# Loading the second sketch matrix through another engine's queue, and moving one group of products within the prologue

## Chip, cores and metric

One core of one Trainium2 chip. The metric is device time in microseconds (us) of one execution, the median of several. Most executions of one kernel agree within 0.3%; now and then one takes 193 to 196 us. These are called slow here and are left out of the comparisons.

## The reference, cut to what matters

```python
def phi(x):                                  # 64 features from two sketches of 8
    a = np.einsum('rd,bhsd->bhsr', S1, x)    # S1, S2: (8, 32)
    b = np.einsum('rd,bhsd->bhsr', S2, x)
    return np.einsum('bhsi,bhsj->bhsij', a, b).reshape(*x.shape[:-1], 64)
q_p, k_p = phi(q), phi(k)                    # q, k, v: (4, 4, 1088, 32)
kv, z = k_p^T v, sum(k_p)
attn = (q_p kv) / (q_p z + 1e-6)
x = attn.transpose(0, 2, 1, 3).reshape(4352, 128)
out = relu(x @ w_in)**2 @ w_out              # w_in (128, 2048), w_out (2048, 128)
```

Nothing can be computed before S1 and S2 are in SBUF: k and q both pass through them.

## The kernel before

Nearly all of the time is the feed-forward part, which TensorE does for chunk after chunk of tokens. Ahead of it stands a prologue for batch 0: load S1, S2 and the first pieces of k, q and v; turn the sketch matrices (`s_T`); compute k features (`kf`, two or three tiles of 128 tokens at a time); sketch 256 tokens of q in two steps (`q0(0)`, `q0(1)`); sum k features against v (`kvp`); divide; and feed the first tokens to the feed-forward part (`pg`, line L615). While the loads are under way, TensorE runs ten products on constants (`warm`), so that its clock is up when real work comes.

```python
    nc.vector.memset(s_nat[:], 0.0)
    nc.scalar.dma_start(s_nat[0:8, :], S1[:, :])        # L214
    nc.scalar.dma_start(s_nat[8:16, :], S2[:, :])       # L215
    load_k(nc.sync, 0, 0, 512)
    load_k(nc.sync, 0, 512, S)
    load_q(nc.sync, 0, 0, 256)
    ...
    load_v(nc.sync, 0, 0, 0, 4)
    load_v(nc.scalar, 0, 2, 0, 4)
    load_v(nc.sync, 0, 1, 0, 4)
    load_v(nc.scalar, 0, 3, 0, 4)
    ...
    keep_warm(W0)                                       # W0 = 10
    a_kT0(0, 4)                                         # VectorE transposes k, first chunk
    nc.vector.transpose(s_T[:, :], s_nat[:, :])         # L706, needs S1 and S2
    ...                                                 # copies of s_T into sf and sq
    a_kf(0, 2, psf, "po")
    a_kf(2, 2, psf, "pg")
    a_kf(4, 3, psf, "po")
    q0(0)
    q0(1)
    nc.scalar.copy(_ap(qb0, ...), banks(x0, 0, 0, 256))
    st[0, "kvp"] = psf.tile([128, 512], F32, tag="pg", name="kvp")
    for t0, n in ((0, 2), (2, 2), (4, 3), (7, 2)):
        a_kp0(t0, n)                                    # VectorE: kp = outer product of kf
        for t in range(t0, t0 + n):
            a_kv0(t)                                    # TensorE: kvp
        if t0 == 0:
            a_kf(7, 2, psf, "po")
```

## Time and profile before

| | before |
|---|---|
| first three runs | 189.06, 189.63, 195.55 us |
| profiled run | 189.23 us, span 187.4 us |
| TensorE busy | 182.0 us, 97% |
| prologue, to the first L615 product | 14.17 us |
| after it | TensorE never idle to speak of |

A line of the chain of waits gives start, duration and what ran; the chain is the work that ended last, followed back. A line of the timeline gives start, duration, engine, line, operation, and in square brackets how long the engine had been idle and what ended that. VectorE's timeline at the end of the k features:

```profile
9.62 0.69 DVE L322 TENSOR_TENSOR kp<-kf,kb 128x512 f32<-128x512 f32 x1 [1.21 <-ACT kb L312]
10.23 0.68 DVE L767 TENSOR_TENSOR qp<-x,qb 128x512 f32<-128x512 f32 x1
11.17 0.49 DVE L780 TENSOR_TENSOR bd<-kvp,own_p 128x128 f32<-128x128 f32 x2 [0.26 <-PE kvp L376]
```

VectorE waits 1.21 us for the last k features, which the change addresses.

### The profile page before, as it was taken

The numbers are of one execution on the slowest core, as the hardware profiler recorded it, in microseconds if no ns is written. First come the engines' busy times: TensorE is split into PE (matmuls) and PEld (weight loads), VectorE is DVE, ScalarE is ACT, GpSimd is POOL, SyncE is SP. The second block draws the span as 40 slices with busy tenths as digits, with TensorE's granted clock in tenths as the row PEclk, the third lists the DMA queues.
The fourth block names the chain that finished last, engine by engine and source line by source line (L and its number), as shares of the span: only waits on it lengthen the run. The fifth ranks groups of instructions, "written<-read, shape, count | busy, mean of one in ns | idle before, by whom it ended". The sixth has DMA issues, their size and how long they took to land.

```text
span 187.4 us, 4142 instructions
## 1 busy us (share of the span) xinstructions
PE 182.0 (97%) x1586; PEld 121.8 (65%) x1587; DVE 115.0 (61%) x261; ACT 149.4 (80%) x329; POOL 28.0 (15%) x125
## 2 busy tenths in 40 slices
PE   8999999999999999999999999999999999999991
PEld 2757866666656666656577666656577655666890
DVE  4779879958992589469944589469943412222400
ACT  3418778778978989789698989789698998999960
POOL 2832000028400000085000000085000000000000
PEclk9999999999999999999999999999999999999998
DMA  6799400100039600200069200200020200020101
GB/s 189 189 344 325 125 3 2 28 3 5 0 50 251 143 6 0 44 1 2 7 146 251 35 3 0 42 3 0 7 41 0 35 0 2 9 43 0 31 11 28
DMA packets 24411, 11.27 MB, mean 60 GB/s; under 512 B 17864, under 2 KB 22728, under 8 KB 24392
## 3 DMA queue, kind: packets, MB, share of 16 engines
q1 hardware_dynamic: 23940, 10.82, 23.7%
q8 instruction: 12, 0.20, 0.4%
q10 hardware_dynamic: 452, 0.20, 0.4%
q14 instruction: 7, 0.06, 0.1%
HBM read 8.78 MB, written 2.23 MB: 59 GB/s over the span
## 4 chain that ended last, share of the span: by engine, by line
PE 94%; DMA 2%; DVE 1%; issue 0%; ACT 0%; POOL 0%; ACTq 0%; DVEq 0%
PE po L653 60%; PE pg L615 18%; PE nd L538 3%; PE kvp L394 2%; PE pol L648 2%; PE po L648 2%; PE qc L296 2%; DMA s_nat<-in_S_dram 2%; PE kvp L376 1%; PE kf L306 1%; PE kc L296 1%; PE x L749 1%; PE nd L547 1%; PE den L795 0%; PE den L773 0%
## 5 line engine op out<-in xcount | busy, mean ns | idle before, releaser
L653 PE MATMUL po<-g,w_o 128*128 128x384 f32 (+3 forms) x352 | 138.4, 478 | 0.0
L615 PE MATMUL pg<-xT,w_in 128*128 128x384 f32 (+3 forms) x192 | 110.1, 582 | 0.3 <-DVE xT L810 0.3
L624 ACT ACTIVATE gt<-pg 128x384 f32<-128x384 f32 (+4 forms) x177 | 85.2, 489 | 20.0 <-PE pg L615 16.9
L653 PEld LDWEIGHTS po<-g,w_o 128*128 128x128 f32 x352 | 62.6, 189 | 22.3 <-issue 7.3
L632 ACT ACTIVATE g<-gt 128x384 f32<-128x384 f32 (+3 forms) x138 | 71.0, 532 | 2.9
L615 PEld LDWEIGHTS pg<-xT,w_in 128*128 128x128 f32 x192 | 36.0, 190 | 25.1 <-issue 7.2
L634 DVE TENSOR_TENSOR g<-gt 128x384 f32<-128x384 f32 (+4 forms) x39 | 21.4, 550 | 39.5 <-ACT gt L624 39.4
L443 POOL COPY kv<-kvt 32x64 f32<-32x64 f32 x48 | 11.8, 246 | 89.7 <-PE po L653 63.9
L506 DVE STREAM_SHUFFLE qa<-qc 128x576 f32<-128x576 f32 (+2 forms) x20 | 11.6, 650 | 0.0
L521 DVE TENSOR_TENSOR qp<-qa,qb 128x576 f32<-128x576 f32 (+2 forms) x20 | 10.8, 601 | 0.0
L497 POOL COPY rd<-rc 32x9 f32<-32x9 f32 x48 | 8.9, 185 | 2.2
L347 DVE TENSOR_TENSOR kp<-fs 128x576 f32<-128x576 f32 x12 | 8.2, 741 | 0.0
L469 DVE STREAM_TRANSPOSE qt<-qc 128x576 f32<-128x576 f32 x6 | 4.3, 762 | 5.5 <-PE qc L296 5.5
L657 DVE STREAM_TRANSPOSE oT<-po 128x384 f32<-128x384 f32 (+3 forms) x11 | 6.2, 560 | 1.2 <-PE po L653 1.2
L538 PE MATMUL nd<-qp,kv 32*32 32x288 f32 (+2 forms) x320 | 6.8, 353 | 0.0
L338 DVE STREAM_TRANSPOSE fs<-kc 128x576 f32<-128x576 f32 x6 | 4.3, 762 | 3.9 <-PE kc L296 3.9
L538 PEld LDWEIGHTS nd<-qp,kv 32*32 32x32 f32 x320 | 3.8, 103 | 3.5 <-issue 2.1
L584 DVE TENSOR_TENSOR xT<-nd,bc 128x576 fp32r<-128x576 f32 (+2 forms) x10 | 5.6, 596 | 0.8 <-PE nd L538 0.7
L506 DVE STREAM_SHUFFLE qb<-qc 128x576 f32<-128x576 f32 (+2 forms) x10 | 6.0, 648 | 0.0
L696 PE MATMUL warm<-const-bfloat16-1.0 128*128 128x512 bf16 x12 | 5.2, 585 | 0.8 <-PEq L1072 0.8
L289 DVE STREAM_TRANSPOSE qT<-qn 128x192 f32<-128x192 f32 (+3 forms) x11 | 5.8, 562 | 0.0
L575 DVE STREAM_TRANSPOSE bc<-rd 128x576 f32<-128x576 f32 (+2 forms) x10 | 5.7, 603 | 0.1
(98 smaller groups left out, 97.6 us busy)
## 6 DMA issues: line engine op xcount, KB each, us to landing
kn<-in_k_dram SPq DMA_DIRECT2D x3, 544.0 KB, 6.8
qn<-in_q_dram SPq DMA_DIRECT2D x3, 544.0 KB, 6.7
vn<-in_v_dram SPq DMA_DIRECT2D x9, 144.0 KB, 5.3
out_dram<-oT SPq DMA_DIRECT2D x24, 48.0 KB, 1.8
w_in<-in_moe_w_in_dram SPq DMA_DIRECT2D x4, 256.0 KB, 6.5
w_o<-in_moe_w_out_dram SPq DMA_DIRECT2D x4, 256.0 KB, 5.9
out_dram<-oT SPq DMA_DIRECT2D x8, 56.0 KB, 1.9
qn<-in_q_dram SPq DMA_DIRECT2D x1, 416.0 KB, 5.6
```

What stands on the lines that cost most here:

```text
L347: nc.vector.tensor_tensor(out=_ap(st[b, "kp"], 0, 128, 2 * o, [[64, NT], [8, 8], [1, 8]]), in0=_ap(fs, 0, 128, o, [[32, NT], [1, 8], [0, 8]]),
L443: nc.gpsimd.tensor_copy(_ap(st[b, "kv"], 32 * c, 32, 64 * h, [[32, E], [1, 32]]), _ap(st["kvt"], 32 * h, 32, 0, [[64, E], [1, 32]]),)
L497: nc.gpsimd.tensor_copy(st[b, "rd", 0][32 * h : 32 * h + 32, NT * c : NT * c + NT], st[b, "rc"][32 * c : 32 * c + 32, NT * h : NT * h + NT],)
L506: nc.vector.stream_shuffle(in_=banks(st[b, "qc", i0], 2 * x, 0, m), out=_ap(st[b, which, i0], 0, 128, 2 * m * x, [[m, 2], [1, m]]), mask=m ...
L521: nc.vector.tensor_tensor(out=st[b, "qp", i0, e][:, r], in0=st[b, f"qa{e}", i0][:, r], in1=st[b, "qb", i0][:, r], op=mult,)
L538: nc.tensor.matmul(nd[32 * h : 32 * h + 32, 512 * c + col : 512 * c + col + m], kv[r, o : o + 32], qp[r, m * h : m * h + m], start=(e == 0 ...
L615: nc.tensor.matmul(st["pg", u][:, n * i : n * i + n], w_in[:, 128 * (d0 + i) : 128 * (d0 + i) + 128], st[b, "xT"][:, c0 : c0 + n],)
L624: nc.scalar.activation(gt[:, 0:w], st["pg", u][:, 0:w], Relu)
L632: nc.scalar.activation(g2[:, 0:w], gt[:, 0:w], Square)
L634: nc.vector.tensor_tensor(out=g2[:, 0:w], in0=gt[:, 0:w], in1=gt[:, 0:w], op=mult)
L648: nc.tensor.matmul(po[x // 128][:, 0:128], g[:, x : x + 128], w, start=(d == 0), stop=(d == NB - 1),)
L653: nc.tensor.matmul(po[0][:, 0:n], w, g, start=(d == 0), stop=(d == NB - 1))
```

## The change

The intent has two parts. Part 1: S1 and S2 no longer share ScalarE's queue; S2 goes through GpSimd's, so both can start at once. Part 2: the last k features (`a_kf(7, 2)`) are computed between the two q sketches and not after the first `kvp` products, so VectorE gets them sooner.

```diff
-    nc.scalar.dma_start(s_nat[8:16, :], S2[:, :])
+    nc.gpsimd.dma_start(s_nat[8:16, :], S2[:, :])
@@
     q0(0)
+    a_kf(7, 2, psf, "po")
     q0(1)
@@
         for t in range(t0, t0 + n):
             a_kv0(t)
-        if t0 == 0:
-            a_kf(7, 2, psf, "po")
```

## The prediction

> **What bounds the kernel now.** I read the page first. Its busy line and its chain say the same thing.
>
> ```profile
> span 187.4 us, 4142 instructions
> ...
> PE 182.0 (97%) x1586; PEld 121.8 (65%) x1587; DVE 115.0 (61%) x261; ACT 149.4 (80%) x329; POOL 28.0 (15%) x125
> ...
> PE 94%; DMA 2%; DVE 1%; issue 0%; ACT 0%; POOL 0%; ACTq 0%; DVEq 0%
> ```
>
> TensorE carries 94% of the chain that ended last, and nearly all of it is the two feed-forward products (L653 and L615). The change touches none of those: comparing the instruction order of the two kernels, the only differences are in the first 14 us, plus a renumbering of the DMA semaphores. So the second view is busy time by stage, with a cut at 14.17 us, where the first L615 product starts.
>
> ```profile
> 0.00:14.17 14.17, 12.93 (x131) 7.66 (x132) 9.16 (x34) 4.62 (x13) 6.53 (x28) 1.00 0.81 241
> 14.17:24.00 9.83, 9.76 (x153) 7.87 (x154) 8.52 (x33) 8.06 (x16) 0.85 (x2) 1.00 0.74 210
> 24.00:60.00 36.00, 36.00 (x422) 22.02 (x421) 28.60 (x67) 29.25 (x63) 6.76 (x32) 1.00 0.17 38
> ```
>
> (Columns: stretch, length, busy TensorE, weight loads, VectorE, ScalarE, GpSimd.) After 14.17 TensorE is full (9.76 of 9.83, then 36.00 of 36.00). So what the prologue saves shifts everything after it by the same amount; nothing later is waiting to swallow it, and nothing later can be gained.
>
> Third, the chain inside the prologue, in order of time (start, duration):
>
> ```profile
> 1.53 2.89 DMA s_nat<-in_S_dram
> ...
> 4.52 0.21 DVE s_T L706
> ...
> 4.78 0.20 POOL sf L711
> 4.98 0.25 ACT sq L717
> ...
> 5.32 1.75 PE kf L306 x14
> 7.07 1.06 PE x L749 x8
> 8.13 0.61 PE kvp L376 x16
> 8.75 0.59 PE kf L306 x4
> 9.34 1.78 PE kvp L376 x56
> 11.12 0.58 PE den L773 x4
> ```
>
> Two things are to be seen. The sketch matrices decide when real work starts: their load lands at 4.42. Then TensorE goes from 5.32 to 11.12 with nothing but its own work on the chain. Fourth, the timeline shows what stands beside this load.
>
> ```profile
> 0.91 0.59 ACTq L214 DMA_DIRECT2D s_nat<-in_S_dram  x1
> ...
> 1.53 0.30 ACTq L215 DMA_DIRECT2D s_nat<-in_S_dram  x1
> ...
> 3.42 0.71 DVE L283 STREAM_TRANSPOSE kt<-kn 128x512 f32<-128x512 f32 x1 [1.13 <-DMA kn<-in_k_dram]
> ...
> 4.52 0.20 DVE L706 STREAM_TRANSPOSE s_T<-s_nat 32x32 f32<-32x32 f32 x1 [0.38 <-DMA s_nat<-in_S_dram]
> ```
>
> S1 is issued at 0.91, S2 behind it at 1.53. The trace's landing records separate them: S1's last landing is at 3.57, S2's at 4.42. S2, second on the same queue, is the late one. VectorE is idle for only 0.38 us because of it, since it transposes the first k chunk until 4.13.
>
> **What the Trainium skill says.** "DMA: Bandwidth & Descriptors", section "Issuing engines are not separate DMA queues": every queue ends on the same 16 engines, so issuing from another engine saves only sequencer time. Here that is S1's 0.59 us in front of S2, and S2 lands 0.85 us after S1, so the trace agrees that the order of issue costs something, and shows more than the issue time. The same page, section "SWDGE vs HWDGE vs iDMA" with the table "Specifications": the GpSimd queue builds its descriptors in software, with about 1 us to the first byte against about 0.6 us for ScalarE's. The trace of before has no kernel load from GpSimd, so this is untested; for ScalarE's queue it shows 1.71 us from S1's issue to its first packet (0.91 to 2.62), far over 0.6, with the k load moving beside it. "SBUF — State Buffer", section "Who interferes with whom": VectorE in a two-port mode locks GpSimd out of the ports it writes descriptors with. Before 3.42 VectorE runs only memsets here (none after 2.3), so I expect no block. "TensorE: Matmul & The Clock Gate", Part 1: the array runs at half clock until a free-running window of about 3.4 us has been busy. The trace agrees: the ten warm-up products start 0.43 us apart up to 4.57, and two later ones (13.08 and on) load 0.22 us apart; the recorded full clock begins at 5.03.
>
> **Part 1, S2 through GpSimd.** Removed: S2 from behind S1. Added: one load at the head of GpSimd's program, waiting for the 32x32 memset of VectorE that ends at 0.89, so issued near 0.92. How long it takes is the uncertain number. Estimate A: S1's issue-to-landing of 2.66 us (3.57-0.91) plus the page's 0.4 us difference in first byte: 0.92+3.06 = 3.98. Estimate B: the page's fixed 2.0 us for a small GpSimd load ("Anatomy of one DMA"): 2.9. I take 3.8, with 4.4 possible. S1 itself stays at about 3.57.
>
> What it buys is capped by VectorE: the k transpose ends at 4.13, so the transpose of the sketches can start at 4.15 to 4.17 rather than 4.52: 0.36 us. From there to the first kf product was 0.80 us (4.52 to 5.32): a 0.20 us transpose, two copies of 0.17 and 0.24 us on VectorE, and hops. That gives 4.96. The second cap is the warm-up: the tenth warm product starts at 4.57 and takes 0.43 us of the array, to 5.00. So kf starts at 5.00 instead of 5.32: **0.32 us saved**. The other inputs follow: the second k chunk landed at 4.25 and q at 5.06, before the shifted 4.85 and 5.61 at which VectorE wants them; v landed by 5.94 against a need near 8.
>
> GpSimd's memsets (0.31, 0.31, 0.12 us) move behind the load. If the load holds GpSimd 1 to 1.5 us, they end near 3.2, still before its first copy at 4.4. SP's loads were paced by waits on semaphores that S1 and S2 share with later v loads: one v load was issued at 4.44, right after S2 landed. Without S2 on these semaphores it goes near 3.9, and the loads behind it some 0.2 us sooner; all of them land ahead of their use already, so this is worth nothing.
>
> **Part 2, last k features between the two q sketches.** TensorE gets the same instructions in another order: kf 14 passes, sketch one, kf 4, sketch two, kvp 72, rather than kf 14, both sketches, kvp 16, kf 4, kvp 56. I price it from single starts in the trace. Before, the first kf to the first den product is 11.05-5.32 = 5.73 us. For the new order: kf to sketch 1.68 (5.32 to 7.00); sketch one, two pairs 0.32 apart, then 0.31 to the next kind (as 7.76 to 8.06): 0.63; four kf passes 0.16+0.11+0.11, then 0.20 to the next kind: 0.58; sketch two and change-over again 0.63; 72 kvp passes at 0.0292 us, from 1.63/56: 2.10; then 0.15 to den. Sum 5.77, **0.05 us more**: the sketch is split and its slower first pass is paid twice.
>
> What it gives is off the path. VectorE waited for the last k features:
>
> ```profile
> DVE kp L322 <- ACT kb L312: 1.2, 1, 1.2
> ```
>
> That product ran 9.62 to 10.31. In the new order kf ends near 8.3, its copy near 8.5, and the product near 9.2 (all before Part 1's shift). But its consumers, the last 16 kvp passes, began only at about 10.43 anyway; the 56 passes run at 29 ns with no gap, like the first 16. The qp product moves from 10.23 to about 9.3, and its consumer waits for the kvp sum (11.05 and the two bd products) regardless. The new kf needs a PSUM buffer freed by the first kp product at 6.95, and TensorE reaches it at about 7.6, so it does not stall. Part 2 alone: 0 to 0.05 us worse.
>
> **Sum.** -0.32 + 0.05 = -0.27 us, about 0.14%. Undisturbed runs of before gave 189.06, 189.63 and, profiled, 189.23: mean 189.3. Less 0.27 is 189.0; the median quoted for before (189.63) sits higher, so I say 189.1.
>
> **Rivals.** (1) *The GpSimd load lands later than 4.42.* For: software descriptors, the k load on all engines, GpSimd's slower start. Against: 3.5 us between issue and 4.42. At a landing of 4.9 the kernel becomes 0.5 us slower, 189.8. I give it 20%. (2) *Part 2 was the real aim and removes a TensorE stall.* For: VectorE's idle 1.2 us. Against: the gapless kvp passes. If right, with the 0.15 us or so of changing between kinds also saved, 188.8. 10%. (3) *The clock decides.* If the window falls so that the array warms later, the kf passes run at half speed, and part of the early start is lost: gain 0.15 instead of 0.32. It varies by run and not by kernel, so it is noise on both, perhaps 0.5 us. (4) *Earlier loads collide* and delay the w_in chunks: chunk three landed at 13.61 and is wanted after 16, so over 2 us of slack. Under 5%.
>
> **Range and chances.** Spread of before's good runs 0.6 us, the mechanism between -0.6 and +0.5: 188.4 to 189.9 holds 8 in 10. Two per cent is 3.8 us, which is fourteen times the effect; only a median that falls in the slow state (195.55 was seen) gets there, and verdicts leave that out.
>
> **What would show it.** Right: the sketch transpose starts at 4.1 to 4.2 with VectorE idle before it under 0.1 us or waiting for nothing; first kf near 5.0; kf to den 5.75 to 5.8; the last kp product with no idle before it; first L615 product near 13.9. Wrong: that transpose waits for the S2 load past 4.4; or kf to den shrinks below 5.6; or TensorE idles before the four kf passes; or the stretch from the first L615 product to the end changes by more than 0.3 us.

## The result, and the profile after

| | before | after |
|---|---|---|
| median | 189.32 us (6 runs) | 189.75 us (6 runs) |
| fast runs | 189.06 to 189.63 | 189.52 to 189.89 |
| ratio of fast runs | | 1.0024, interval 1.0010 to 1.0038 |
| span of the profiled run | 187.40 | 187.73 |
| last landing of S2 | 4.42 | 4.50 |
| sketch transpose starts | 4.52 | 4.52 |
| first `kf` product | 5.32 | 5.32 |
| first `kf` to first `den` | 5.73 | 5.90 |
| first `den` to first L615 | 3.12 | 3.12 |
| first L615 to last product | 168.89 | 168.91 |
| last landing of output to end of span | 0.96 | 1.10 |

Ratios are the mean time of one kernel's fast runs over that of the other's of the same rounds, so not quite the ratio of the medians. The change is within 2% and inside the predicted range, but its sign is the other way: 0.24% slower, where 0.14% faster was forecast.

The chain of waits of the changed kernel:

```profile
0.90 0.35 issue
1.25 3.25 DMA s_nat<-in_S_dram
4.50 0.02 issue
4.52 0.21 DVE s_T L706
...
5.32 1.87 PE kf L306 x14
7.19 0.63 PE x L749 x4
7.83 0.59 PE kf L306 x4
8.41 0.63 PE x L749 x4
9.05 2.25 PE kvp L376 x72
11.29 0.58 PE den L772 x4
```

The first line is new: between the end of VectorE's memset and the start of GpSimd's load lie 0.35 us in which nothing that the profile shows is waited for. The load then takes 3.25 us where S2 on ScalarE's queue took 2.89, so the 0.28 us of earlier issue (1.25 against 1.53) are gone, and the transpose starts at 4.52 as before. The rest runs as in the prediction's list of the new order: 0.63, 0.59, 0.63, 2.25. Only the first entry differs, 1.87 for 1.75.

VectorE's timeline of the changed kernel:

```profile
4.52 0.20 DVE L706 STREAM_TRANSPOSE s_T<-s_nat 32x32 f32<-32x32 f32 x1 [0.34 <-DMA s_nat<-in_S_dram]
...
8.70 0.69 DVE L322 TENSOR_TENSOR kp<-kf,kb 128x512 f32<-128x512 f32 x1 [0.18 <-ACT kb L312]
9.71 0.69 DVE L766 TENSOR_TENSOR qp<-x,qb 128x512 f32<-128x512 f32 x1 [0.32 <-ACT qb L760]
11.34 0.49 DVE L779 TENSOR_TENSOR bd<-kvp,own_p 128x128 f32<-128x128 f32 x2 [0.94 <-PE kvp L376]
```

The sketch transpose still waits for the load of S2. Part 2 does what it was meant to: the wait of 1.21 us is 0.18. It comes back two lines on, as a wait of 0.94 us for `kvp`; `bd` starts 0.17 us later than before.

Busy time by stage of the changed kernel, with the cut at its first L615 product (length, TensorE, weight loads, VectorE, ScalarE, GpSimd):

```profile
0.00:14.34 14.34, 13.13 (x130) 7.65 (x132) 9.35 (x34) 4.62 (x13) 7.40 (x29) 1.00 0.84 241
14.34:24.17 9.83, 9.77 (x153) 7.87 (x154) 8.52 (x33) 8.05 (x16) 0.62 (x1) 1.00 0.82 207
24.17:60.17 36.00, 36.00 (x422) 22.02 (x421) 28.63 (x67) 29.26 (x63) 6.81 (x32) 1.00 0.17 38
```

TensorE is as full as before. Matched product by product, the two kernels stand 0.18 us apart from the middle of `kvp` to the last product. So the 0.33 us of this pair of profiles are 0.18 in the prologue and 0.14 after the last product.

Three causes were in question. A: the route through GpSimd (a later S2, and something at the program's end). B: the new order on TensorE. C: chance, because the array's clock became full at 5.03 us in the one profile and at 5.58 in the other.

### The profile page after: what moved, and what is told of

It reads as the page before. It is cut to its first block, busy times and chain, and to the rows that moved or that the text cites. A ratio compares the mean times of both kernels' runs of the same rounds, so it can differ in the third digit from the quotient of the medians.

```text
span 187.7 us, 4143 instructions
## 1 busy us (share of the span) xinstructions
PE 182.2 (97%) x1586; PEld 121.8 (65%) x1587; DVE 115.2 (61%) x261; ACT 149.5 (80%) x329; POOL 28.8 (15%) x126
## 4 chain that ended last, share of the span: by engine, by line
PE 94%; DMA 2%; DVE 1%; issue 1%; ACT 0%; POOL 0%; DVEq 0%
PE po L653 60%; PE pg L615 18%; PE nd L538 3%; PE kvp L394 2%; PE pol L648 2%; PE po L648 2%; DMA s_nat<-in_S_dram 2%; PE qc L296 2%; PE kf L306 1%; PE kvp L376 1%; PE kc L296 1%; PE x L749 1%; PE nd L547 1%; PE den L794 0%; PE den L772 0%
## 5 line engine op out<-in xcount | busy, mean ns | idle before, releaser
L615 PE MATMUL pg<-xT,w_in 128*128 128x384 f32 (+3 forms) x192 | 110.1, 582 | 0.3 <-DVE xT L809 0.3
L615 PEld LDWEIGHTS pg<-xT,w_in 128*128 128x128 f32 x192 | 36.0, 190 | 25.1 <-issue 6.3
```

The source lines that it names most:

```text
L615: nc.tensor.matmul(st["pg", u][:, n * i : n * i + n], w_in[:, 128 * (d0 + i) : 128 * (d0 + i) + 128], st[b, "xT"][:, c0 : c0 + n],)
```

## The experiments

All gave correct results. Ratios are to the kernel before, from the same rounds.

| run | edit to the kernel before | median, us | ratio | interval |
|---|---|---|---|---|
| e1 | Part 1 alone | 189.62 | 1.0016 | 1.0003 to 1.0029 |
| e2 | Part 2 alone | 189.25 | 0.9997 | 0.9984 to 1.0011 |
| e3 | S2 on SyncE | 189.46 | 1.0010 | 0.9998 to 1.0023 |
| e4 | both parts, again | 189.64 | 1.0019 | 1.0006 to 1.0032 |
| e6 | S2 on SyncE, q on ScalarE | 190.16 | 1.0052 | 1.0010 to 1.0093 |
| e9 | a useless load on GpSimd | 189.11 | 0.9993 | 0.9981 to 1.0005 |
| e5 | loads in a quiet stretch | 189.61 | one run | |
| e10 | S2 and all v on SyncE | 189.16 | 0.9995 | 0.9983 to 1.0008 |
| e11 | all v on SyncE | 189.17 | 1.0000 | 0.9988 to 1.0012 |
| e12 | as e11, S2 on GpSimd | 189.71 | 1.0023 | 1.0008 to 1.0037 |
| e13 | both parts, 12 warm-up products | 189.80 | 1.0035 | 1.0020 to 1.0050 |
| e14 | both parts, 7 warm-up products | 194.09 | 1.0236 | 1.0198 to 1.0274 |

### One part at a time: e1, e2, and both again: e4

```diff
 e1:
-    nc.scalar.dma_start(s_nat[8:16, :], S2[:, :])
+    nc.gpsimd.dma_start(s_nat[8:16, :], S2[:, :])
 e2: only the move of a_kf(7, 2, psf, "po")
 e4: the changed kernel, unedited
```

> Part 1 alone (S2 on GpSimd's queue, old order of TensorE). Theory A (the load through GpSimd lands as late as before, near 4.4 to 4.6 us, and the program's end grows by 0.1 to 0.15 us because a further DMA semaphore is waited for and drained): sketch transpose at 4.45 to 4.65, first kf at 5.25 to 5.45, from the last TensorE product to the end of the span 0.1 to 0.15 us longer than before; ratio 1.0005 to 1.002. Theory B (the order of TensorE's work is what costs): ratio 1.000 and this run looks like before. Theory C (only the phase of TensorE's clock differed): the time equals before within noise and the end of the span is unchanged.

> Part 2 alone (last k features between the sketches, S2 still on ScalarE's queue). Theory A: from the first kf product to the first den product 0.05 us longer than before if the clock is full for both, sketch transpose at 4.5, end of the span unchanged; ratio 1.000 to 1.001. Theory B: 0.2 us or more longer and a ratio of 1.0015 or more. Theory C: ratio 1.000.

> The changed kernel once more, beside the others. Theory A: ratio 1.001 to 1.003; landing of S2 again at 4.4 to 4.6 and the end of the span 0.1 to 0.15 us longer; the start of TensorE's full clock differs from 5.58 us. Theory C: ratio within 0.999 to 1.001, with the difference following the start of full clock.

Part 1 alone has a ratio of 1.0016, Part 2 alone 0.9997, both again 1.0019. So Part 1 carries the loss, and theory B falls. Theory C, chance, cannot be the whole of it either: e1, e4 and e12, all with S2 on GpSimd, each have an interval wholly above 1, and chance would strike on both sides. The chain of e1:

```profile
1.24 3.47 DMA s_nat<-in_S_dram
...
4.74 0.21 DVE s_T L706
```

S2 lands at 4.71, and the sketch transpose starts 0.22 us later than before. At the end of the program, e1 needs 1.10 us from the last landing to the end of the span, as the changed kernel does, where before needs 0.96.

The chain of e2:

```profile
5.24 1.75 PE kf L306 x14
6.98 0.63 PE x L749 x4
7.62 0.59 PE kf L306 x4
8.21 0.63 PE x L749 x4
8.84 2.25 PE kvp L376 x72
11.09 0.58 PE den L772 x4
```

With the clock full from the start, as in before, the first `kf` to the first `den` takes 5.78 us by single starts, against 5.73: the 0.05 us of the prediction, too small for the timed runs to see. e4's profile fell in the slow state; its four other runs gave the ratio, and its profile is used further on.

### Is an early S2 worth 0.32 us? e3, e6, e10, e11

```diff
 e3:
-    nc.scalar.dma_start(s_nat[8:16, :], S2[:, :])
     load_k(nc.sync, 0, 0, 512)
+    nc.sync.dma_start(s_nat[8:16, :], S2[:, :])
     load_k(nc.sync, 0, 512, S)
 e6: as e3, and
-    load_q(nc.sync, 0, 0, 256)
+    load_q(nc.scalar, 0, 0, 256)
 e10: as e3, and load_v(nc.scalar, ...) -> load_v(nc.sync, ...), both
 e11: only load_v(nc.scalar, ...) -> load_v(nc.sync, ...), both
```

> S2 on SyncE's queue after the first k chunk, S1 alone on ScalarE's, old order of TensorE: tests the step of the prediction that an S2 that lands early is worth 0.32 us. If that step holds: S2 lands near 3.8, sketch transpose at 4.15 to 4.25, first kf at 5.0, first L615 product near 13.85, ratio 0.998 to 0.999. If something else caps it (the second k chunk, now issued 0.3 us later, or the half-speed clock that a kf at 5.0 meets), first kf at 5.0 but the first L615 product at 14.0 or later, ratio 0.9995 or more.

> S2 on SyncE's queue behind the first k chunk, and the first q chunk moved to ScalarE's queue behind S1, ahead of v, so that neither q nor the second k chunk is pushed behind v as in the run before. If early sketch matrices are worth what the prediction said once nothing else is late: second k chunk by 4.8, q by 5.5, sketch transpose at 4.2, first kf near 4.95, first L615 product near 13.85, ratio 0.9975 to 0.999. If any reshuffle of the first loads only moves the lateness from one input to another: k or q again lands later than VectorE wants it, first L615 product at 14.1 or later, ratio 0.9995 or more.

> S2 on SyncE's queue behind the first k chunk, and every v load on SyncE's queue behind q, so that ScalarE's queue carries S1 alone and nothing overtakes the second k chunk and q. If the early sketch matrices are worth the 0.32 us of the prediction when nothing else is late: second k chunk by 4.7, q by 5.5, sketch transpose at 4.2, first kf near 4.95, first L615 product 13.8 to 13.9, ratio 0.998 to 0.999. If the 1 KB load itself holds up the k chunk behind it: k after 4.9, ratio 0.9995 or more.

> Control for the run above: the kernel before with all v loads on SyncE's queue behind q, S1 and S2 both on ScalarE's as before. Expected under every theory: sketch transpose at 4.4 to 4.5, first kf near 5.25 to 5.35, ratio 0.9985 to 1.0005; a ratio as low as that of the run above would mean that moving v is the gain and not S2.

In e3 S2 lands at 3.63, the sketch transpose starts at 4.17 and the first `kf` at 4.93, as the prediction's two caps had it. Yet the first L615 product comes at 14.38, later than before. VectorE's timeline of e3 shows why:

```profile
4.17 0.16 DVE L706 STREAM_TRANSPOSE s_T<-s_nat 32x32 f32<-32x32 f32 x1
...
5.39 0.84 DVE L283 STREAM_TRANSPOSE kt<-kn 128x384 f32<-128x384 f32 x2 [0.61 <-DMA kn<-in_k_dram]
6.50 0.45 DVE L289 STREAM_TRANSPOSE qT<-qn 128x256 f32<-128x256 f32 x1 [0.26 <-DMA qn<-in_q_dram]
```

The second k chunk landed at 5.37 (before: 4.25) and q at 6.47 (before: 5.06). The k chunk was issued 0.39 us later, but it landed 1.12 later. ScalarE's queue, relieved of S2, now issues v at the same moment (1.60). Where v is moved away, in e10 below, k lands at 5.06 and q at 5.51: the company of v goes with 0.31 us of k's delay and 0.96 of q's, and the other 0.81 of k's with its place behind S2. e6 turned that around the wrong way: q on ScalarE's queue beside k, and the k chunk, issued at 1.62, landed at 6.35; first L615 product at 14.99. Its ratio of 1.0052 is also raised by a fast run of 191.73 us with a mean clock of only 0.989.

e10 leaves ScalarE's queue with S1 alone. S2 lands at 3.64, k at 5.06, q at 5.51, and the timeline of its TensorE begins the work at the predicted time:

```profile
4.99 2.06 PE L306 MATMUL kf<-sf,kt 128*128 128x64 f32 x14
6.98 1.13 PE L749 MATMUL x<-qT,sq 64*128 64x256 f32 x8
```

But from the first `kf` to the first q sketch it takes 1.99 us, where before took 1.68: in this profile the clock became full only at 5.79, so the early products ran at half speed, and the sketches start at 6.98 against 7.00. Its six runs go from 188.70 to 189.47 us. Two of them, 188.70 and 188.71, lie under every run of the control e11 (189.11 to 189.26); only one run has a trace. On average e10 gains 0.05%, which is not distinguishable from nothing. This is what its expectation said for a k chunk after 4.9 (it landed at 5.06), but TensorE did not wait for k: once the clock is full, its `kf` passes start 0.11 us apart, as in before.

The record says a little more of the clock. It has each run's mean granted clock, and in all 14 traces the clock changes a whole number of times 3.413 us apart (before: full at 5.03, half at 185.94, which is 53 times; e14, further down: once and twice). So a mean below 1 gives the time of the last change to half clock, and from that, to about 0.2 us, when the clock became full. This is an estimate; for the profiled runs of before and e10 it gives 4.99 and 5.74 where the traces have 5.03 and 5.79. The run of 188.70 has a mean of 0.995: full near 4.1, ahead of its first `kf`. Three others of e10 (189.10, 189.22, 189.27) have 0.998: full near 5.6 to 5.8. For 188.71 and 189.47 the mean is 1.000, which leaves it open. Before's three runs of the same rounds with 0.995 took 188.95 to 189.27. So with the clock full in time an early S2 may well be worth its 0.32 us; one run does not show it. The same reading explains much of the spread of before's own fast runs: the five with 0.998 took 189.36 to 189.56 us, the sixteen with 0.994 to 0.997 took 188.95 to 189.32.

### What the GpSimd route costs: e9, e5, e12

```diff
 e9:
     nc.scalar.dma_start(s_nat[8:16, :], S2[:, :])
+    nc.gpsimd.dma_start(scr[0:8, :], S2[:, :])      # nobody reads scr
 e5: three such loads by GpSimd and three by ScalarE, in the middle of the kernel
 e12: as e11, and
-    nc.scalar.dma_start(s_nat[8:16, :], S2[:, :])
+    nc.gpsimd.dma_start(s_nat[8:16, :], S2[:, :])
```

> The kernel before, with one more load: S2 a second time, by GpSimd at the head of its program, into a tile that nobody reads and with no wait ahead of it. Separates the two costs of Part 1. Theory A1 (the end of the program pays for having used GpSimd's queue at all): last landing to end of span 1.09 us instead of 0.96, ratio 1.0005 to 1.0015, sketch transpose at 4.4 to 4.6 as before. Theory A2 (all of the cost is the later landing of S2): end unchanged, ratio 1.000. It also shows how soon GpSimd's load starts without a wait (0.75 to 0.85 us if the wait for VectorE's memset was the delay, 1.2 if it was not) and when it lands.

> The kernel before, with three more 1 KB loads of S2 by GpSimd and three by ScalarE in the middle of the kernel, where the DMA engines are nearly idle, into a tile that nobody reads; the time itself is not of interest. If GpSimd's route has a fixed cost of its own: issue to last landing 0.5 us or more longer than by ScalarE, near 2.5 to 3 us against 2. If only the crowd of first loads made it late: both within 0.3 us of each other, near 2 us.

> As the control, but with S2 on GpSimd's queue: Part 1 of the change with no v load on ScalarE's queue beside it. If the crowd of v packets on ScalarE's queue held GpSimd's load back: S2 lands by 4.2, sketch transpose at 4.2, ratio 0.998 to 0.9995. If the delay is in the route (issue at 1.25, packets at 3.5, completion 0.7 us or more after the last packet): lands at 4.45 or later again, ratio 1.0005 to 1.002.

e9 has both routes in one execution. Its timeline:

```profile
0.92 0.59 ACTq L215 DMA_DIRECT2D s_nat<-in_S_dram  x1
...
1.25 0.64 POOL L217 DMA_DIRECT2D scr<-in_S_dram  x1 [0.80 <-POOLq L1074]
...
1.54 0.30 ACTq L216 DMA_DIRECT2D s_nat<-in_S_dram  x1
```

GpSimd's load waits for nothing here and still starts at 1.25: the 0.35 us were not the wait for VectorE's memset. Whether the instruction or only its record starts that late is not shown; the landings do not depend on it. From the trace's landing records:

| S2 by | run | issued | last data packet starts | last landing | issue to landing |
|---|---|---|---|---|---|
| ScalarE | before | 1.53 | 3.79 | 4.42 | 2.89 |
| ScalarE | e2 | 1.54 | 3.69 | 4.33 | 2.79 |
| ScalarE | e9 | 1.54 | 3.72 | 4.33 | 2.79 |
| ScalarE | e11 | 1.54 | 3.84 | 4.46 | 2.92 |
| GpSimd | after | 1.25 | 3.80 | 4.50 | 3.25 |
| GpSimd | e1 | 1.24 | 3.72 | 4.71 | 3.47 |
| GpSimd | e9 | 1.25 | 3.73 | 4.61 | 3.36 |
| GpSimd | e12 | 1.24 | 3.93 | 4.76 | 3.52 |

Both routes put the data on the engines at the same time, near 3.4 to 3.9, so the earlier issue is already lost there. GpSimd's completion then comes 0.70 to 0.99 us after the last data packet starts, ScalarE's 0.61 to 0.64. The traces left out of the table widen this: by GpSimd, e13, e14 and the slow e4 took 3.52, 3.21 and 3.67 us to land, 1.03, 0.65 and 1.08 of it after the last packet started; by ScalarE, e5 took 2.91, with 0.70. So GpSimd's flight is the longer one in all seven traces that have it (3.21 or more against 2.92 or less), but in e14 its completion is not. One visible difference: GpSimd's load is signalled by 16 landings, the ScalarE load of eight rows by eight. That the last of sixteen comes later than the last of eight fits, but was not tested by itself. e12 removes the v loads from ScalarE's queue and S2 still lands at 4.76; its ratio of 1.0023 stands beside 1.0000 for the control e11. So the neighbours on ScalarE's queue are not what holds it.

e5 asks for the same in a quiet stretch. Per load, issue to last landing: by ScalarE 1.27 and 1.44 us (the third met another burst of loads and is left out), by GpSimd 1.70, 2.47 and 1.69. So the route costs some 0.25 to 0.43 us by itself (1.0 or more for the load of 2.47), and the crowd at the start adds 1.4 to 2 us to either route.

At the end of the program, from the last landing of the output to the end of the span, kernels without a GpSimd load take 0.96 to 0.97 us (before, e2, e3, e6, e10, e11); those with S2 on GpSimd 1.09 to 1.10 (after, e1, e4, e12, e13, e14); e9 takes 1.04, e5 with three such loads 1.20. In the changed kernel 0.06 of it is one further semaphore that SyncE looks at, because the semaphores of all later loads moved round by one, and 0.07 is GpSimd's own final drain and clearing of semaphores. e9, which pays 0.07 here and lands S2 as before, is not slower (0.9993), but its interval is too wide to show or deny so little. The 0.14 us of the end are less than half of Part 1's loss. What makes the rest is seen best in e11 and e12, which differ in Part 1 alone and whose profiles have the clock full at 4.25 and 4.11, well before the first `kf`:

| | e11 | e12 | difference |
|---|---|---|---|
| last landing of S2 | 4.46 | 4.76 | 0.30 |
| first `kf` product | 5.36 | 5.58 | 0.22 |
| first L615 product | 14.21 | 14.43 | 0.22 |
| last product starts | 183.10 | 183.32 | 0.22 |
| last landing of output | 186.42 | 186.72 | 0.30 |
| end of span | 187.39 | 187.82 | 0.43 |

So of 0.43 us, which is also what the ratios 1.0000 and 1.0023 say, 0.22 is the later S2, 0.14 the end of the program, and 0.08 a later landing of the output, whose cause is open (in before and after it differs by 0.01).

### What the slow runs are: e13, e14

```diff
-    W0, W3 = 10, 3
+    W0, W3 = 12, 3     # e13; e14: 7, 3
```

e4's profile is of a slow run. Its chain:

```profile
5.74 3.22 PE kf L306 x14
...
12.32 4.04 PE kvp L376 x72
```

The same fourteen products take 3.22 us and not 1.75, the 72 take 4.04 and not 2.25: half speed. The recorded full clock begins at 16.51 us. TensorE had been idle from the end of the warm-up to 5.74; from there on it is called busy, and yet two whole stretches of 3.413 us (6.27 to 13.10, counted back from 16.51) pass at half clock.

> The changed kernel with twelve warm-up products instead of ten. Tests whether the runs near 195 us are those in which TensorE's clock was not full before the small prologue products began (in the slow profile of the changed kernel it became full only at 16.5 us, after an idle gap of TensorE between the warm-up's end and a first kf at 5.74). If so: no slow run in six here, since the warm-up now reaches 5.4 to 5.9 and leaves no gap; fast runs 0.1 to 0.5 us longer than the changed kernel's, ratio to before 1.003 to 1.005. If the slow state is something else: about one run in five slow as for the other kernels with S2 on GpSimd's queue.

> The changed kernel with seven warm-up products: TensorE is idle from about 3.9 to 5.3. If the slow runs are missed warm-ups: at least half of the six runs near 193 to 196 us, and where a profile shows it, full clock only after 12 us. If the slow state is something else: at most two of six, and fast runs as for the changed kernel, ratio 1.001 to 1.003.

With seven products all six runs lie between 192.36 and 194.70 us (they carry the label fast only because none of that kernel was faster). With twelve, none of four runs was slow, and the fast ones cost 0.35% rather than 0.2%: the first `kf` starts at 5.78, where e12, with S2 landing at 4.76 too and ten products, starts at 5.58. Busy time by stage of e14, whose last columns are clock, DMA share and GB/s:

```profile
7.70:14.00 6.30, 6.30 (x82) 5.42 (x84) 2.13 (x4) 0.80 (x2) 3.51 (x11) 0.50 0.99 311
```

The clock in the records is 0.50 while TensorE is called busy throughout. It had been full from 4.24 to 7.65, and fell back: one stretch of 3.413 us at full clock, then two at half. So the one slow execution with a trace is one whose warm-up was missed, and taking warm-up away makes every run slow. That the other slow runs are the same is likely; they have no trace, and four runs of e13 without a slow one do not show it. The kernel before was slow in 3 of 40 runs, the four kernels with S2 on GpSimd and ten warm-up products (after, e1, e4, e12) in 5 of 23. A later first `kf` leaves a longer gap, so more slow runs would follow; the counts are too small to call that shown.

## Why the prediction was right or wrong

The range held (189.75 in 188.4 to 189.9), but by its width and not by the mechanism: it reached past zero on both sides, and the forecast gain of 0.27 us came as a loss of 0.24%, some 0.45 us. The prediction's own sign of being wrong appeared: the sketch transpose waits for S2 past 4.4 (VectorE is idle for 0.34 us, until 4.52). By its steps:

- *After 14.17 TensorE is full, so the prologue's gain or loss passes through unchanged.* Right: 168.89 and 168.91 us from the first L615 product to the last.
- *Part 2: 0.05 us more; VectorE's wait is off the path.* Right in mechanism and size: 5.78 against 5.73 in e2. The freed 1.2 us returned as a wait for `kvp`.
- *"Issued near 0.92", "I take 3.8, with 4.4 possible" for S2's landing.* This is the step that failed. GpSimd's load is on record as issued at 1.25 with or without a wait (0.33 us lost), and it takes 3.21 to 3.67 us to land where estimate A had 3.06 and estimate B 2.0. It landed at 4.50, and in e1 and e12 at 4.71 and 4.76, against 4.42 before; that the transpose of the profiled run starts no later than before is the better end of this spread. Estimate B was the cost of a load in quiet (1.7 in e5), taken for one in a crowd. Rival 1 was what happened; I gave it 20%.
- *The saving is capped by VectorE and the warm-up at a first `kf` of 5.00.* Right as to the time (4.93, 4.99 and 4.99 in e3, e6 and e10), not shown as to its worth. "The other inputs follow" held for the change itself, but getting S2 in early pushed k and q back in e3 and e6, and in the profile of e10 the clock took the gain; the run of 188.70 suggests that the gain is there when the clock is full in time.
- *Rival 3, the clock decides, as noise.* Right that it takes part of an early start: the half-speed stretch cost 0.12 us of the profile after and 0.31 in e10, where the rival allowed 0.17. It is not noise on both kernels alike: the earlier the first `kf`, the more of it a late clock can take. 0.12 of the 0.33 us between the first two profiles are this chance, and not the change.
- *The end of the program.* Missing from the sum: 0.13 to 0.14 us.

For the profile after, the terms add up: S2 0.00, clock 0.12, order 0.05, end 0.14, together 0.31 of 0.33. In the timed runs, which average over the clock, Part 1 makes 0.30 us (0.16% in e1), from a later S2 and the end. In e12 against e11 the shares are 0.22 and 0.14; run by run they stay open, since only one run of each kernel has a trace.

## What to carry to other kernels

Before moving a small load to another queue for an earlier start, compare issue to landing of that route in the same crowd, not its issue time: 0.28 us of earlier issue was more than lost in 0.4 to 0.6 us of longer flight. Where several inputs gate the start, an input that comes early is worth only what the next late one leaves, and moving a 1 KB load can delay a big one by more than the time by which it is issued later (1.12 us for 0.39 in e3). An engine's wait that vanishes is no gain if its consumer waits for another engine.

## What the Trainium skill lacked or had wrong

- "DMA: Bandwidth & Descriptors", section "Anatomy of one DMA — SWDGE (gpsimd) path": a fixed cost of about 2.0 us. In quiet 1.69 to 2.47 us here, but 3.21 to 3.67 us while the first loads fill the engines; ScalarE's route likewise went from 1.27 and 1.44 up to 2.79 to 2.92. A figure for such a crowded start is missing, and so are figures for the completion, which came 0.65 to 1.08 us after the start of GpSimd's last packet against 0.61 to 0.70 for ScalarE's.
- No page has a figure for how late a first load on GpSimd's queue starts: on record at 1.25 with no wait (e9), where in before GpSimd's first instruction of this part (the memset of `sq`, with no load ahead of it) starts at 0.73. The record's start may lag the instruction's.
- No page has the cost at the program's end of having used GpSimd's queue: 0.96 us became 1.09 to 1.10.
- "TensorE: Matmul & The Clock Gate", section "Part 1: The HAM clock gate (the "warmup" mystery)": full clock comes after one window of about 3.4 us in which TensorE is busy. Here being called busy was not enough: in e4 TensorE is called busy from 5.74 on and the clock is full only at 16.51. In e14 the clock fell to half at 7.65 and stayed there to 14.47, with TensorE called busy since 5.28 and a gap of only some 1.4 us before; six of six runs lost 3 to 5.5 us. That the small fp32 products count for less than the warm-up products is a guess that fits; no run tests it.
